# Gated mix of linear attention and a gated MLP: phi(k)'s sums by accumulating transfers, the gate's logits turned by VectorE, x's second chunk loaded later

## The chip, the cores and the metric

The kernel runs on one core of a Trainium2 chip. A core has TensorE (PE, matrix products into PSUM), VectorE (DVE), ScalarE (ACT), GpSimd (POOL) and SyncE (SP); here GpSimd and SyncE mainly issue transfers (DMAs) for the 16 DMA engines. Each engine executes its own queue in order, and waits on semaphores for the others. The metric is the device time of one execution in microseconds, the median of several runs. Next to it stands one profiled execution, in which every instruction has a start and a duration.

## The reference

Only `A_x` (2048 tokens x 640) is used as input x of both branches. Cut to what matters:

```python
x = A_x
g = sigmoid((x * gate_w).sum(-1, keepdims=True))     # one gate logit for each token
q, k, v = split(x @ wqkv)                            # 32 heads of 20 columns each
phi = lambda t: where(t > 0, t + 1, exp(t)) + 1e-6
kv = einsum("bhsd,bhse->bhde", phi(k), v)
z = phi(k).sum over the tokens                       # one number for each head and column
num = einsum("bhqd,bhde->bhqe", phi(q), kv)
den = einsum("bhqd,bhd->bhq", phi(q), z) + 1e-6
a = (num / den).reshape(1, 2048, 640) @ wo
b = (sigmoid(x @ w_gate) * (x @ w_up)) @ w_down      # 1536 inner columns
return g * a + (1 - g) * b
```

All is float32. The result is handed over transposed, as `out_t`.

## The kernel before

**Products.** Each float32 operand is split into a high and a low part (`split`: ScalarE copies the high part, VectorE subtracts it), and a product is three matmuls: high by high, high by low, low by high (`mm3`, lines 200 to 202; nearly all rows of TensorE carry one of these lines). The large products with x go by a scheme of Strassen's kind: seven products of half blocks instead of eight, on sums of quarters of x (`Chunk.sum`, `Chunk.form`, the forms `xt0` to `xt3`) and of the weights (`queue_w`: pieces G, U, S, V). `Chunk.sum(3)` and `Chunk.form(3)` make the fourth form of x.

**Stages.** (1) Up to about 145 us: k for all tokens in blocks of 128, phi(k), and G^T = x^T phi(k) into `gt`. Along the way `phi` copies one column of the product, the gate's logit, into `logit` (128 tokens by 16 blocks), and `z_add` adds the block of phi(k) to `zacc` (128 x 640) with an accumulating transfer from GpSimd's queue. (2) 145 to about 228 us: q for the two pairs of token groups (`QLast`, `QBlock`), phi(q) (`phi_q`, stored to `p_dram`), and between the blocks' steps the list `parts`: for six groups of heads `kv_part` (kv from `gt` and wv, then VectorE masks and splits it: kvt, kvh, kvl), `m_part` (kv times wo into `ms`, stored to `m_dram`), and the small work on z and the logits. `m_close` then frees the memory of this stage (`kp` with `gt` and `zacc`, `m1`, `mp`) and loads x of pair 0 again into tiles that lie there (`hf`). (3) The gated MLP's first half in 12 blocks, with the denominators made beside it (`begin`, `den`: they use `zcol` and `zeps`). (4) The second half, with kv wo as further rows of w_down.

**z and the logits before.** `z_perm` (part 2): VectorE adds the epsilons to `zacc` and permutes its columns. `z_part` (part 6): five products of `zperm` with a column of ones, line 1083, sum over the 128 partitions into the five columns of `zcol`; VectorE copies them and makes `zeps`, their sum by partition. `turn_logits` (part 2): line 1091 turns `logit` by a product with the identity `ident`, ScalarE copies it to `lt`, and GpSimd stores it to `l_dram`, from which the gates are later read by rows (`gate_row`).

**Order.** The program is unrolled, and its order is written out by hand with a planner's help. `Order` keeps estimated clocks for TensorE, ScalarE and VectorE; work is queued with estimated costs, a `ready` time and a key, and `fill` puts queued work between the matmuls when the clocks say that it fits; `need(key)` forces it. `step(blk, s)` runs step s of a block and then fills. Work that a DMA brings has an estimated due time (`est`, `later`). The DMA queues follow from this order: SyncE's carries the loads, GpSimd's the stores and accumulates. Tiles with the same tag share a ring of buffers: `ke`, `lt` and most `ms` share `ma` (two), `xnst`, every third `wv_sb`, `zperm` and every third `ms` share `mb` (two).

**Loads in stage 2.** `load_mv` brings a group's columns of wv, `load_mo` rows of wo (line 1068), `load_x1` the second chunk of x of pair 0 (`xst`, line 335); the last one is queued with a condition on how many groups of wv have been asked for:

```python
order.add(0, 0, load_x1, None, lambda: 0.0 if 3 in MV else 1e9)
```

Of the kernel before, what the change touches and what calls it, by code (L numbers as in the profile page):

```python
# [7 lines left out]
F32 = mybir.dt.float32  # L8
# [7 lines left out]
P = 128  # L16
# [161 lines left out]
def gated_mix_kernel(ctx: ExitStack, tc: tile.TileContext, xt, xn, wk, wv, wo, wst_q, wst_f, out_t):  # L178
# [64 lines left out]

    zcol = common.tile([P, KC], F32, name="zcol")
    zeps = common.tile([P, 1], F32, name="zeps")
    logit = common.tile([P, S // P], F32, name="logit")
    p_dram = dram.tile([P, KC, NG, TG], F32, name="p_dram")
    mp_dram = dram.tile([P, KC, D], F32, name="mp_dram")
    m_dram = dram.tile([D, D], F32, name="m_dram")
# [2 lines left out]
    h_dram = {(pr, n): dram.tile([P, FC // 2 + 2, TG], F32, name=f"h{pr}{n}") for pr in range(2) for n in FORMS}  # L252
    d_dram = [dram.tile([H, 2, TG], F32, name=f"d{i}") for i in range(2)]
    f_dram = dram.tile([P, TG], F32, name="f_dram")
    s_dram = [dram.tile([P, 2, TG], F32, name=f"s{p}") for p in range(FC // 2 + 2)]
    r_dram = [dram.tile([P, 2, TG], F32, name=f"r{pr}") for pr in range(2)]
    bdn = HPG * DH


    common.tile([P, 56], F32, name="space")  # L260

    kp_cm = tc.tile_pool(name="kp", bufs=1)
    kp = kp_cm.__enter__()
    gt = kp.tile([P, KC, D], F32, name="gt")
    ident = kp.tile([P, P], F32, name="ident")
    ones_f = kp.tile([P, P], F32, name="ones_f")
    bd = kp.tile([HPG * DH, HPG, DH], F32, name="bd")
    zacc = kp.tile([P, D], F32, name="zacc")
# [55 lines left out]
    class Chunk:  # L324
# [54 lines left out]
        def queue_sums(self, first=True, last=True):  # L379
            w = 2 * self.w  # L380
            plan = [(0, ()), (1, ()), (2, ((1, 3), (0, 4), (2, 5)))] if first else []
            for n, forms in plan + ([(3, ((3, 6),))] if last else []):
                order.add(0, v_cost(w), lambda n=n: self.sum(n), None, lambda: self.at)
                for t, k in forms:
                    order.add(a_cost(w), v_cost(w), lambda t=t: self.form(t), self.key(k))

        def queue(self, sums=True):
            self.queue_a()
# [239 lines left out]
    def z_add(r):  # L628

        nc.gpsimd.dma_start(zacc.rearrange(view2, j=2), r, accum_op=OP.add if z_started else OP.bypass)  # L630
        z_started.append(1)

    def queue_split(b):
        for s in range(2):
            order.add(a_cost(D), v_cost(D), lambda s=s: k_split(tok(b, s)), ("pk", b))
# [73 lines left out]
        W[n, piece] = [t[:, c] for c in range(2)]  # L709
        split(*W[n, piece], src)  # L710

    def queue_w(n, between=None, early=False):


        def raw(i, k0, k1):
            return WST[n][:, i, k0 * P:k1 * P]

        def g_part():
            w_form(n, "G", raw(0, 0, KC))
            if n[0] == "u":  # L720
                order.then(load_w)

        def sums(part):
            if part == 0:
                add(raw(1, 2, 4), raw(1, 0, 2), raw(1, 2, 4))
                sub(raw(1, 0, 2), raw(0, 0, 2), raw(1, 0, 2))
            else:
                sub(raw(0, 0, 2), raw(1, 2, 4), raw(0, 0, 2))
                sub(raw(0, 2, 4), raw(0, 2, 4), raw(0, 0, 2))
                sub(raw(0, 4, 5), raw(0, 4, 5), raw(1, 4, 5))  # L730

        def form_u():
            w_form(n, "U", raw(1, 2, KC))

        if early:
            order.add(a_cost(3 * P), v_cost(3 * P), form_u, None, lambda: max(W_AT.get(n, 1e9), w_free("U")))
            order.add(0, 2 * v_cost(2 * P), lambda: sums(0))
            return
        order.add(a_cost(D), v_cost(D), g_part, ("G", n),
                  lambda: max(W_AT.get(n, 1e9), w_free("G")))  # L740
        if n[0] != "u":
            if between:
                between()
            else:
                order.add(a_cost(3 * P), v_cost(3 * P), form_u, None, lambda: max(W_AT.get(n, 1e9), w_free("U")))
                order.add(0, 2 * v_cost(2 * P), lambda: sums(0))
            order.add(0, 3 * v_cost(2 * P), lambda: sums(1))
            order.add(a_cost(D), v_cost(D), lambda: w_form(n, "S", raw(0, 0, KC)), ("S", n),
                      lambda: w_free("S"))

# [26 lines left out]
    for k in range(2, KC):  # L777
        b1.k(k)
        if k == 2:
# [4 lines left out]
            split_xn(1)  # L784


    ij = p1.tile([P, HW], F32, name="ij", tag="ta", bufs=2)[:, :P].bitcast(I32)
    nc.gpsimd.memset(ones_f, 1.0)
    nc.gpsimd.iota(ij, pattern=[[1, P]], base=P, channel_multiplier=-1)
    nc.gpsimd.affine_select(bd, ones_f[:bdn, :bdn].rearrange("p (b c) -> p b c", c=DH),  # L790
                            pattern=[[-DH, HPG], [0, DH]], base=0, channel_multiplier=1,
                            compare_op=OP.is_ge, fill=0.0)
    nc.gpsimd.affine_select(bd, bd, pattern=[[DH, HPG], [0, DH]], base=DH - 1, channel_multiplier=-1,
                            compare_op=OP.is_ge, fill=0.0)

    def constants():
        vec1(ident, ij, float(P), op0=OP.is_equal)


    order.pe = max(order.pe, order.vec)  # L800
# [14 lines left out]
    for c in range(1, 4):  # L815
        ck = chunks[c]
        if c == 1:
            a, b = KPlain(2), KPlain(3)
            order.need((ck, "plain"))
            queue_ks()  # L820
            queue_xn(2)
            for k in range(KC):
                a.k(k)
                order.fill()
            a.phi_a()
            for k in range(KC):
                b.k(k)
                order.fill()
                if k == 0:
                    a.phi_b()  # L830
                    order.add(0, 0.6, constants)
            order.need(("ks", 5))
            for t in range(2):
                k_split(tok(2, t))
        else:
            a, b = KBlock(2 * c), KBlock(2 * c + 1)
            for n in range(1, 6):
                order.need((ck, n))
                if c == 2 and n >= 3:
                    order.need(("ks", (1, 0, 2)[n - 3]))  # L840
                getattr(a, f"s{n}")()
                getattr(b, f"s{n}")()
                if n == 2:
                    queue_xn(2 * c)
            order.need((ck, 6))
            if c == 2:
                order.need(("ks", 5))
            if c + 1 < len(chunks):
                chunks[c + 1].load()
            else:  # L850
                nx = [Chunk(0, i, None, xst_v) for i in range(2)]
                nx[0].load()
            a.s6()
            a.s7()
            a.sum_b()
            a.phi_a()
            b.s6()
            a.phi_b()
            order.need(("pk", 2 * c - 1))
            k_split(tok(2 * c, 0))  # L860
            b.s7()
            b.sum_b()
            k_split(tok(2 * c, 1))
# [30 lines left out]
        for u in range(2 * KC):  # L894
            g.part(u, 3 if u < 4 else 0, 4)
            order.fill()
    order.need(("xn", 7))
    glast = GTBatch(4, [7])
    tags = ["rot", "rot", "dd", "dd", "ch", "ch", "cc", "cc", "rot", "rot"]

    for u in range(4):
        glast.part(u, 0, 2, tags[u])
    for u in range(4, 10):
        glast.part(u, 0, 2, tags[u], out=False)
        order.fill()
    p1_tail = [lambda u=u: glast.out(u) for u in range(4, 10)]
    p1_cm.__exit__(None, None, None)

# [30 lines left out]
    class Block:  # L939
# [18 lines left out]
        def s1(self):  # L958
            order.need(("G", self.n))
            self.ch = ch_tile()  # L960
            prod(self.ch, self.terms("G", (0, 1), self.a(0, 1)), True)
            self.dd = ps_tile("dd")
            prime(self.dd)
            act(self.dd, self.ch, AF.Copy, "q" if self.n == ("q", 2) else "p")

        def s2(self):
            prod(self.dd, self.terms("G", (2, 3, 4), self.a(2, 3, 4)), False)
# [101 lines left out]
            MO[hg] = o  # L1069
            MO_AT[hg] = order.pe + 5.0  # L1070

    ZP = []

    def z_perm():
        zperm = m1_tile("mb", "zperm")
        ZP.append(zperm)
        vec1(zperm.rearrange("p (d h) -> p d h", h=H), zacc.rearrange("p (h d) -> p d h", d=DH), S // P * EPS, op0=OP.add)

    def z_part():
        zperm = ZP[0]  # L1080
        zps = ps_tile("ch")
        for u in range(KC):
            nc.tensor.matmul(zps[:, u:u + 1], zperm[:, u * P:(u + 1) * P], ones_f[:, 0:1], start=True, stop=True)
        vec_copy(zcol, zps[:, :KC], "p")
        nc.vector.tensor_reduce(zeps, zcol, op=OP.add, axis=mybir.AxisListType.X)
        vec1(zeps, zeps, EPS)

    def turn_logits():

        ps = ps_tile("rot")  # L1090
        nc.tensor.matmul(ps[:S // P, :P], logit, ident, start=True, stop=True)
        t = m1.tile([P, D], F32, name="lt", tag="ma", bufs=2)[:S // P, :P]
        act(t, ps[:S // P, :P], AF.Copy, "p")
        nc.gpsimd.dma_start(l_dram, t)

    def wo_split(hg):
        _, w = hg_slice(hg)
# [85 lines left out]
    def gate_row(g, rows=P):  # L1183
# [2 lines left out]
    nt = Chunk(0, 0, XF[0], None, TG)  # L1186


    parts = [[lambda: kv_part(0)], [lambda: kv_part(1), z_perm, turn_logits], [lambda: kv_part(2)],
             [lambda: kv_part(3), lambda: m_part(0)], [lambda: kv_part(4), lambda: m_part(1)],  # L1190
             [lambda: kv_part(5), z_part, lambda: m_part(2)], [lambda: m_part(3)], [lambda: m_part(4)],
             [lambda: m_part(5), m_rows, m_close]]

    def part():
# [28 lines left out]
    def load_x1():  # L1223
        nx[1].load(est=7.0)
        nx[1].later = 3.0
    order.add(0, 0, load_x1, None, lambda: 0.0 if 3 in MV else 1e9)
    nx[1].queue_a()
    nx[1].queue_b()
    order.stream = order.items
# [12 lines left out]
    for n, b in enumerate(blocks):  # L1242
# [11 lines left out]
        if n != 1:  # L1254
            queue_su({0: ("q", 1), 2: ("q", 2), 3: ("f", 0)}[n])
        if n == 1:
            queue_w(("q", 2), lambda: nt.queue_sums(first=False))
        elif n == 2:
            queue_w(("u", 0))
            queue_w(("f", 0))  # L1260
# [110 lines left out]
            order.late.append((max(order.pe, order.vec) + 1.0, lambda: den_sum(half, 0)))  # L1371

    def begin():
        st["a"], st["b"] = h_tile(), h_tile()
        load_pair(0)
        load_pair(1)
# [515 lines left out]
```

## Time and profile before

| what | us |
|---|---|
| median of 3 runs | 733.09 |
| lowest and highest run | 732.86, 735.78 |
| the profiled execution | 731.36 |
| its span, first to last instruction | 729.6 |
| TensorE busy | 723.1 (99%) |
| VectorE busy | 487.3 (67%) |
| ScalarE busy | 319.8 (44%) |
| GpSimd busy | 119.3 (16%) |

Matmuls overlap in the records: one of 512 columns shows about 0.39 us, and the next starts 0.23 us after it, so times on TensorE are counted from start to start. A row of the order of time gives start, duration, engine, line, operation, what is written and read, its shape and count, and in brackets how long the engine was idle before and what released it. `SPq` rows are issues by SyncE's queue. TensorE's granted clock is 0.999 of full speed over the span.

### The profile page before, as it was taken

The numbers are of one execution on the slowest core, as the hardware profiler recorded it, in microseconds if no ns is written. First come the engines' busy times: TensorE is split into PE (matmuls) and PEld (weight loads), VectorE is DVE, ScalarE is ACT, GpSimd is POOL, SyncE is SP. The second block draws the span as 40 slices with busy tenths as digits, with TensorE's granted clock in tenths as the row PEclk, the third lists the DMA queues.
The fourth block names the chain that finished last, engine by engine and source line by source line (L and its number), as shares of the span: only waits on it lengthen the run. The fifth ranks groups of instructions, "written<-read, shape, count | busy, mean of one in ns | idle before, by whom it ended". The sixth has DMA issues, their size and how long they took to land.

```text
span 729.6 us, 9792 instructions
## 1 busy us (share of the span) xinstructions
PE 723.1 (99%) x3552; PEld 619.5 (85%) x3552; DVE 487.3 (67%) x787; ACT 319.8 (44%) x540; POOL 119.3 (16%) x207
## 2 busy tenths in 40 slices
PE   9999999999999999999999999999999999999997
PEld 7999999988878888888888888888888888888886
DVE  4878566867764688678879868795856764434340
ACT  5764627156766324233423342233356654424320
POOL 0211010111311023212224223240200000010000
PEclk9999999999999999999999999999999999999999
DMA  8453537587636454755587658475887965465432
GB/s 265 116 137 88 154 54 233 111 257 263 206 131 222 152 195 130 206 187 199 213 280 276 237 182 286 164 260 161 282 315 260 341 220 198 154 214 191 150 113 73
DMA packets 61941, 143.67 MB, mean 197 GB/s; under 512 B 10798, under 2 KB 23870, under 8 KB 61893
## 3 DMA queue, kind: packets, MB, share of 16 engines
q1 hardware_dynamic: 43685, 88.50, 37.8%
q0 software_dynamic: 18064, 54.42, 22.8%
q8 instruction: 28, 0.46, 0.3%
q14 instruction: 20, 0.16, 0.1%
q10 hardware_dynamic: 144, 0.13, 0.1%
HBM read 89.73 MB, written 49.68 MB: 191 GB/s over the span
## 4 chain that ended last, share of the span: by engine, by line
PE 96%; DMA 2%; DVE 1%; ACT 1%; issue 0%; SPq 0%; DVEq 0%
PE ch L202 9%; PE ch L201 9%; PE ch L200 9%; PE cc L200 9%; PE cc L201 8%; PE cc L202 8%; PE rot L200 8%; PE rot L201 8%; PE rot L202 8%; PE dd L200 6%; PE dd L201 6%; PE dd L202 6%; DMA wo_sb<-wo 1%; DMA xnh<-wk 0%; DVE wol L216 0%; ACT woh L212 0%
## 5 line engine op out<-in xcount | busy, mean ns | idle before, releaser
L216 DVE TENSOR_TENSOR hf<-hw,hf 128x1024 fp32r<-128x1024 f32 x54 | 65.9, 1223 | 68.9 <-ACT hf L212 68.5
L212 ACT ACTIVATE hf<-hw 128x1024 fp32r<-128x1024 f32 x54 | 56.9, 1057 | 62.3 <-PE rot L202 31.2
L216 DVE TENSOR_TENSOR c<-cc,c 128x512 f32<-128x512 f32 x56 | 37.8, 686 | 45.7 <-PE cc L202 41.3
L212 ACT ACTIVATE wG<-wst 128x640 fp32r<-128x640 f32 x17 | 12.4, 737 | 65.0 <-PE dd L202 65.0
L212 ACT ACTIVATE c<-ch 128x512 f32<-128x512 f32 x32 | 19.1, 598 | 49.3 <-PE ch L202 44.5
L1688 POOL DMA_DIRECT2D out_t<-ot x18 | 9.7, 541 | 182.4 <-DVE ot L216 179.3
L200 PE MATMUL dd<-xrh,wG 128*128 128x512 f32 x90 | 35.6, 395 | 0.0
L202 PE MATMUL dd<-xrh,wG 128*128 128x512 f32 x90 | 35.0, 389 | 0.0
L201 PE MATMUL dd<-xrl,wG 128*128 128x512 f32 x90 | 35.0, 389 | 0.0
L216 DVE TENSOR_TENSOR c<-c,om 128x512 f32<-128x512 f32 x48 | 33.2, 692 | 1.7
L200 PE MATMUL cc<-xbh,wS 128*128 128x512 f32 x84 | 32.8, 390 | 0.1
L201 PE MATMUL cc<-xbl,wS 128*128 128x512 f32 x84 | 32.7, 389 | 0.0
L202 PE MATMUL cc<-xbh,wS 128*128 128x512 f32 x84 | 32.7, 389 | 0.0
L200 PE MATMUL rot<-pkh,xnh 128*128 128x320 f32 x102 | 31.7, 310 | 0.0
L201 PE MATMUL rot<-pkl,xnh 128*128 128x320 f32 x102 | 31.5, 309 | 0.0
L202 PE MATMUL rot<-pkh,xnl 128*128 128x320 f32 x102 | 31.4, 308 | 0.0
L200 PE MATMUL dd<-hf,wa 128*128 128x512 f32 x80 | 31.1, 389 | 0.0
L201 PE MATMUL dd<-hf,wa 128*128 128x512 f32 x80 | 31.1, 389 | 0.0
L202 PE MATMUL dd<-hf,wa 128*128 128x512 f32 x80 | 31.1, 389 | 0.0
L200 PE MATMUL ch<-hf,wa 128*128 128x512 f32 x80 | 31.1, 389 | 0.0
L201 PE MATMUL ch<-hf,wa 128*128 128x512 f32 x80 | 31.1, 389 | 0.0
L202 PE MATMUL ch<-hf,wa 128*128 128x512 f32 x80 | 31.1, 389 | 0.0
(471 smaller groups left out, 2211.5 us busy)
## 6 DMA issues: line engine op xcount, KB each, us to landing
hf<-p_dram SPq DMA_DIRECT2D x16, 512.0 KB, 4.7
hw<-h1T SPq DMA_DIRECT2D x16, 512.0 KB, 4.9
hw<-h0T SPq DMA_DIRECT2D x16, 512.0 KB, 4.6
wst<-wst_f SPq DMA_DIRECT2D x12, 640.0 KB, 4.3
xst<-xt SPq DMA_DIRECT2D x10, 640.0 KB, 7.0
h1T<-c POOLq DMA_DIRECT2D x24, 256.0 KB, 2.7
h0T<-c POOLq DMA_DIRECT2D x24, 256.0 KB, 3.5
hw<-h1B SPq DMA_DIRECT2D x11, 512.0 KB, 4.5
```

The lines of the kernel that those rows point to most:

```text
L200: nc.tensor.matmul(out, l_hi, r_hi, start=first, stop=False, skip_group_check=True)
L201: nc.tensor.matmul(out, l_hi, r_lo, start=False, stop=False, skip_group_check=True)
L202: nc.tensor.matmul(out, l_lo, r_hi, start=False, stop=last, skip_group_check=True)
L212: nc.scalar.activation(out, src, fn, **kw)
L216: nc.vector.tensor_tensor(out, a, b, op=op)
L1688: (eng or nc.gpsimd).dma_start(out_t[o * P:(o + 1) * P, g * TG + c0:g * TG + c1], t[:, c0:c1])
```

## The change

1. *z*: the tile `zperm`, `z_perm` and `z_part` go. In their place `z_step`, called nine times, works off a list: seven accumulating transfers add the upper half of the rows that are left of `zacc` to the lower half (64 rows, 32, down to 1), an eighth call stores row 0 to `z_dram`, a ninth loads it by four transfers into the five columns of `zcol`. All are issued by GpSimd. The calls stand after the fifth and ninth product of the third batch's last loop, after the second, sixth and tenth of the last batch, and in parts 1, 2, 3 and 5. `z_done`, at the start of stage 3, adds the epsilons and makes `zeps`.
2. *Logits*: the identity and the instructions that make it go. `logit` is 32 columns wide (the upper 16 are zeros); VectorE turns its four blocks of 32 x 32 at once, and four transfers instead of one store them.
3. *x's second chunk*: `load_x1` waits for the fifth group of wv to be asked for, not the fourth; it moves behind the loads of wo and wv of that part.
4. *Order of the group ("q", 2)*: x's fourth sum stays ahead of the weights' last three sums, the fourth form is queued behind them.
5. The copy in `Block.s1` names the pair too in its condition for the wait "q". The tile `space` shrinks by as much as `logit` grows.

```diff
-    logit = common.tile([P, S // P], F32, name="logit")
+    logit = common.tile([P, 32], F32, name="logit")
+    z_dram = dram.tile([1, D], F32, name="z_dram")
-    common.tile([P, 56], F32, name="space")
+    common.tile([P, 40], F32, name="space")
-    ident = kp.tile([P, P], F32, name="ident")
...
+        def queue_sum3(self):
+            order.add(0, v_cost(2 * self.w), lambda: self.sum(3), None, lambda: self.at)
+
+        def queue_form3(self):
+            order.add(a_cost(2 * self.w), v_cost(2 * self.w), lambda: self.form(3), self.key(6))
...
+    z_tree = [64, 32, 16, 8, 4, 2, 1, 0, -1]
+
+    def z_step():
+        n = z_tree.pop(0)
+        if n > 0:
+            nc.gpsimd.dma_start(zacc[:n], zacc[n:2 * n], accum_op=OP.add)
+        elif n == 0:
+            nc.gpsimd.dma_start(z_dram, zacc[0:1])
+        else:
+            for d in range(4):
+                nc.gpsimd.dma_start(zcol[d * H:(d + 1) * H], z_dram.rearrange("o (h u d) -> (o d) h u", u=KC, d=4)[d])
...
-    def queue_w(n, between=None, early=False):
+    def queue_w(n, between=None, early=False, third=None):
...
             order.add(0, 3 * v_cost(2 * P), lambda: sums(1))
+            if third:
+                third()
             order.add(a_cost(D), v_cost(D), lambda: w_form(n, "S", raw(0, 0, KC)), ("S", n),
...
-    ij = p1.tile([P, HW], F32, name="ij", tag="ta", bufs=2)[:, :P].bitcast(I32)
+    nc.gpsimd.memset(logit[:, S // P:], 0.0)
-    nc.gpsimd.iota(ij, pattern=[[1, P]], base=P, channel_multiplier=-1)
-    def constants():
-        vec1(ident, ij, float(P), op0=OP.is_equal)
-                    order.add(0, 0.6, constants)
...
             g.part(u, 3 if u < 4 else 0, 4)
             order.fill()
+            if c == 3 and u in (4, 8):
+                z_step()
...
         glast.part(u, 0, 2, tags[u])
+        if u == 1:
+            z_step()
     for u in range(4, 10):
         glast.part(u, 0, 2, tags[u], out=False)
         order.fill()
+        if u in (5, 9):
+            z_step()
...
-            act(self.dd, self.ch, AF.Copy, "q" if self.n == ("q", 2) else "p")
+            act(self.dd, self.ch, AF.Copy, "q" if (self.pr, self.n) in ((0, ("q", 2)),) else "p")
...
-    def z_perm():
-        zperm = m1_tile("mb", "zperm")
-        vec1(zperm.rearrange("p (d h) -> p d h", h=H), zacc.rearrange("p (h d) -> p d h", d=DH), S // P * EPS, op0=OP.add)
-    def z_part():
-        for u in range(KC):
-            nc.tensor.matmul(zps[:, u:u + 1], zperm[:, u * P:(u + 1) * P], ones_f[:, 0:1], start=True, stop=True)
-        vec_copy(zcol, zps[:, :KC], "p")
+    def z_done():
+        vec1(zcol, zcol, S * EPS, op0=OP.add)
         nc.vector.tensor_reduce(zeps, zcol, op=OP.add, axis=mybir.AxisListType.X)
         vec1(zeps, zeps, EPS)
 
     def turn_logits():
-        ps = ps_tile("rot")
-        nc.tensor.matmul(ps[:S // P, :P], logit, ident, start=True, stop=True)
-        t = m1.tile([P, D], F32, name="lt", tag="ma", bufs=2)[:S // P, :P]
-        act(t, ps[:S // P, :P], AF.Copy, "p")
-        nc.gpsimd.dma_start(l_dram, t)
+        t = m1.tile([P, D], F32, name="lt", tag="ma", bufs=2)[:, :32]
+        nc.vector.transpose(t, logit)
+        order.on_vec(32, "")
+        for r in range(0, P, 32):
+            nc.gpsimd.dma_start(l_dram[:, r:r + 32], t[r:r + S // P])
...
-    parts = [[lambda: kv_part(0)], [lambda: kv_part(1), z_perm, turn_logits], [lambda: kv_part(2)],
-             [lambda: kv_part(3), lambda: m_part(0)], [lambda: kv_part(4), lambda: m_part(1)],
-             [lambda: kv_part(5), z_part, lambda: m_part(2)], [lambda: m_part(3)], [lambda: m_part(4)],
+    parts = [[lambda: kv_part(0), z_step], [lambda: kv_part(1), turn_logits, z_step], [lambda: kv_part(2), z_step],
+             [lambda: kv_part(3), lambda: m_part(0)], [lambda: kv_part(4), lambda: m_part(1), z_step],
+             [lambda: kv_part(5), lambda: m_part(2)], [lambda: m_part(3)], [lambda: m_part(4)],
              [lambda: m_part(5), m_rows, m_close]]
...
-    order.add(0, 0, load_x1, None, lambda: 0.0 if 3 in MV else 1e9)
+    order.add(0, 0, load_x1, None, lambda: 0.0 if 4 in MV else 1e9)
...
-            queue_w(("q", 2), lambda: nt.queue_sums(first=False))
+            queue_w(("q", 2), nt.queue_sum3, third=nt.queue_form3)
...
     def begin():
+        z_done()
```

More of the change, by code (lines that the diff above doesn't have):

```diff
@@ L1070, in load_mo @@
             MO_AT[hg] = order.pe + 5.0
-    ZP = []
-    def z_perm():
-        zperm = m1_tile("mb", "zperm")
-        ZP.append(zperm)
-        vec1(zperm.rearrange("p (d h) -> p d h", h=H), zacc.rearrange("p (h d) -> p d h", d=DH), S // P * EPS, op0=OP.add)
-    def z_part():
-        zperm = ZP[0]
-        zps = ps_tile("ch")
-        for u in range(KC):
-            nc.tensor.matmul(zps[:, u:u + 1], zperm[:, u * P:(u + 1) * P], ones_f[:, 0:1], start=True, stop=True)
-        vec_copy(zcol, zps[:, :KC], "p")
+    def z_done():
+        vec1(zcol, zcol, S * EPS, op0=OP.add)
         nc.vector.tensor_reduce(zeps, zcol, op=OP.add, axis=mybir.AxisListType.X)
```

## The prediction

> **What bounds the kernel.** I read the page first, then TensorE's waits, then the stretch from 136 to 210 us in order of time, because everything the diff touches that TensorE executes lies there.
>
> ```profile
> span 729.6 us, 9792 instructions
> ...
> PE 723.1 (99%) x3552; PEld 619.5 (85%) x3552; DVE 487.3 (67%) x787; ACT 319.8 (44%) x540; POOL 119.3 (16%) x207
> ...
> PE 96%; DMA 2%; DVE 1%; ACT 1%; issue 0%; SPq 0%; DVEq 0%
> ```
>
> TensorE is busy for 723.1 of 729.6 us and holds 96% of the chain that ended last. So only two things can change the time by much: matmuls that are added or removed, and stalls of TensorE. The list of its waits is short:
>
> ```profile
> PE rot L290 <- POOL warm L287: 1.4, 1, 1.4
> PE cc L1114 <- DVE kvl L216: 0.5, 1, 0.5
> PE ch L202 <- DVE wS L216: 0.3, 1, 0.3
> ```
>
> The first is the start of the program. The other two lie in the stretch that the change rearranges. Everything else that the diff moves (VectorE's copies, GpSimd's and SyncE's transfers) counts only if it makes TensorE wait.
>
> **Matmuls removed.** In order of time on TensorE:
>
> ```profile
> 150.95 0.39 PE L1091 MATMUL rot<-ident,logit 128*16 128x128 f32 x2
> 151.27 0.50 PE L200 MATMUL ch<-xbh,wG 128*128 128x512 f32 x1
> 164.54 1.27 PE L1083 MATMUL ch<-ones_f,zperm 128*128 128x1 f32 x10
> 165.67 0.39 PE L200 MATMUL rot<-woh,kvh 120*120 120x320 f32 x1
> ```
>
> Matmuls overlap, so I count from start to next start: the logits' turn costs 151.27 - 150.95 = 0.32 us, the five column sums of z 165.67 - 164.54 = 1.13 us. Together 1.45 us leave TensorE, with nothing put in their place there. On VectorE the permuting of zacc, the copy of zcol and the identity go, a transpose and one small addition come; VectorE is 67% busy and this is under 1 us either way, so I count it as nothing as long as it is not the last to arrive. The change of the copy's wait in the first step of the blocks costs nothing: it names group 2 of q in pair 0, and that group occurs in no other pair.
>
> **x's second chunk is loaded one part later.** The wait for kvl has this history:
>
> ```profile
> 148.39 1.61 SPq L335 DMA_DIRECT2D xst<-xt  x2
> 150.13 1.01 SPq L1068 DMA_DIRECT2D wo_sb<-wo  x2
> 158.12 0.74 ACT L212 ACTIVATE woh<-wo_sb 120x640 fp32r<-120x640 f32 x1 [2.02 <-DMA wo_sb<-wo]
> 158.89 0.82 DVE L216 TENSOR_TENSOR wol<-wo_sb,woh 120x640 fp32r<-120x640 f32 x1 [2.07 <-ACT woh L212]
> 160.56 1.28 PE cc L1114 x10
> ```
>
> The columns are start, duration, instruction (the last row is the chain's). The two loads of x (640 KB each) go out just ahead of two loads of wo; ScalarE then waits for wo, VectorE for ScalarE, and kvt, kvh and kvl queue behind it. How long such a load of wo takes without and with x in front:
>
> ```profile
> wo_sb<-wo SPq DMA_DIRECT2D x1, 300.0 KB, 3.0
> wo_sb<-wo SPq DMA_DIRECT2D x2, 300.0 KB, 8.3
> ```
>
> The first row is the first load of wo in this stretch, ahead of x, the second the pair at 150.13. With x behind wo and the next wv, I expect wo some 4 us earlier, and the wait gone: 0.5 us, plus the restart seen in the gap before 160.56, say 0.6. The ends are 0 (something else holds VectorE there) and 0.7. What is late next is x itself: issued at about 152 instead of 148.4, landing near 160. Its first use by TensorE is the first step of the third block:
>
> ```profile
> 185.28 0.39 PE L200 MATMUL ch<-xah,wG 128*128 128x512 f32 x1
> ```
>
> So there is cover of over 20 us; without it each us would count.
>
> **The order of the third weight group.** The wait for wS:
>
> ```profile
> 200.65 1.23 DVE L216 TENSOR_TENSOR xt3l<-hf,xt3h 128x1024 fp32r<-128x1024 f32 x1 [1.61 <-ACT xt3h L212]
> 201.80 1.08 DVE L216 TENSOR_TENSOR wst<-wst 128x256 f32<-128x256 f32 x3
> 206.21 0.50 PE L202 MATMUL ch<-xt1h,wS 128*128 128x512 f32 x1 [0.31 <-DVE wS L216]
> ```
>
> Today x's fourth form precedes the weight's last sums, and those three (1.08 us) follow it. After the change they come first, and fit into the 1.61 us in which VectorE waits for ScalarE. wS can then be ready some 1 us earlier, and the 0.3 us go. Ends: 0.3 gained, 0.3 lost if the form is now the late one.
>
> **phi(k)'s sums by transfers.** This is where the change can lose. Seven accumulating transfers (64 rows down to 1), a store and four small loads are added to GpSimd's queue; each of the first eight waits for the one before, and whatever is queued behind it on GpSimd waits too. In the order of issue: five steps before the first part, step 6 (2 rows) in the first part, then the first store of phi(q), then four stores of the turned logits in place of one, step 7, the second store of phi(q), step 8 (the store of z), then m's first store. GpSimd's rows today:
>
> ```profile
> 136.30 1.22 POOL L630 DMA_DIRECT2D zacc<-kb  x1 [3.46 <-DVE wG L216]
> 152.73 0.68 POOL L1094 DMA_DIRECT2D l_dram<-lt  x1
> 161.02 0.56 POOL L1135 DMA_DIRECT2D m_dram<-ms  x1 [3.33 <-ACT ms L212]
> ```
>
> Times from issue to landing, in us at the end of each row: of zacc's last sum, of the first store of phi(q) (issued just ahead of l_dram's), of l_dram's and of m's first:
>
> ```profile
> zacc<-kb POOLq DMA_DIRECT2D x1, 320.0 KB, 4.2
> p_dram<-qr POOLq DMA_DIRECT2D x1, 256.0 KB, 7.5
> l_dram<-lt POOLq DMA_DIRECT2D x1, 8.0 KB, 7.1
> m_dram<-ms POOLq DMA_DIRECT2D x1, 300.0 KB, 3.6
> ```
>
> The tree can begin at 136.3 + 4.2 = 140.5. A step of it is shown nowhere. Above it stands an accumulate of 128 KB among other transfers:
>
> ```profile
> 261.39 0.52 POOL L1384 DMA_DIRECT2D d<-hf  x1 [14.00 <-DVE hf L220]
> 266.50 0.86 POOL L1384 DMA_DIRECT2D d<-hf  x1 [0.43 <-DMA d<-hf]
> DMA to landing us min/median/max: 1.7/4.2/6.8
> ```
>
> The first two rows are an issue and the next one that waited for it, 5.1 us later; the third is that tile's summary, with 1.7 us as its shortest. So a step lies between 1.7 and 5.1 us. Its surroundings differ:
>
> ```profile
> 140.00:144.00 4.00, 4.00 (x28) 3.94 (x27) 3.16 (x8) 2.17 (x4) 0.00 (x0) 1.00 0.00 0
> 148.00:152.00 4.00, 4.00 (x24) 3.23 (x23) 3.12 (x7) 2.07 (x5) 0.00 (x0) 1.00 0.98 300
> ```
>
> The last two columns are the DMA engines' busy share and GB/s: idle at first, full later. I take 3.1 us on the average, a us below the 4.2 of the full zacc for fewer bytes. Five steps end at 140.5 + 15.5 = 156.0. Then step 6 and the first store of phi(q) go out, then the four logit stores at some 0.6 us each, until 159.6; behind a store of 256 KB they land near 164 (7.5 us after that store's issue at 156.6, as now).
>
> Who waits for that? The turned logits lie in the buffer that the second group's product ms takes next but one, and ScalarE writes it in the first of these rows (the second comes up below):
>
> ```profile
> 162.37 0.82 ACT L212 ACTIVATE ms<-rot 120x320 f32<-120x320 f32 x2 [0.32 <-ACT xah L212]
> 169.37 0.83 ACT L212 ACTIVATE ms<-rot 120x320 f32<-120x320 f32 x2 [0.63 <-ACT xbh L212]
> ```
>
> Today the logits have landed by 152.73 + 7.1 = 159.8. After the change ScalarE stands at ms until 164, its PSUM buffer is free 0.4 us later, and the next group's product, which would now start at 165.67 less the 2.4 us gained = 163.3, starts at about 164.4: 1.1 us lost. The bounds: 0 with steps under 2.9 us, and 7 us with the last three steps at 5.1 (below).
>
> The price per step has a rule to weigh. The Trainium skill (DMA: Bandwidth & Descriptors, section Anatomy of one DMA — SWDGE (gpsimd) path) gives about 2.0 us fixed plus bytes at 436 GB/s for each such transfer. By that, an estimate, the five steps take 2.4 + 2.2 + 2.1 + 2.05 + 2.0 = 10.8 us, ScalarE waits for nothing and the sum is that of the first rival. The trace so far disagrees: by the same rule zacc's 320 KB would take 2.8 us and its row says 4.2.
>
> Step 8 holds m's first store back until about 165; plus 3.6 it lands at 168.7, when ScalarE, now at 169.37, would want that buffer near 168: under 1 us, hidden by what TensorE then has queued. And x's next pair is loaded into memory that holds zacc:
>
> ```profile
> 166.90 3.99 SPq L335 DMA_DIRECT2D hf<-xt  x4
> 187.30 1.23 DVE L216 TENSOR_TENSOR xt1l<-hf,xt1h 128x1024 fp32r<-128x1024 f32 x1 [1.13 <-ACT xt1h L212]
> 192.76 0.39 PE L200 MATMUL ch<-xt1h,wS 128*128 128x512 f32 x1
> ```
>
> It must now wait for the store of z, which lands near 167. TensorE first uses these forms 192.76 - 188.53 = 4.2 us after they are made, so up to 4 us more would still be covered.
>
> **Sum.** -1.45 (matmuls) - 0.6 (kvl) - 0.3 (wS) + 1.1 (ms) = -1.25 us. It is made on the profiled execution, 731.36 us with a span of 729.6; the median of the runs, 733.09, lies 1.7 above. Taken off the median: 731.8 us.
>
> **Rivals.** *The tree is quick.* With steps at 2.5 us the logits land before 162 and nothing waits: -2.35, 730.7 us. For it speaks the idle DMA at 140 to 144 and the shortest landing of 1.7; against it the full DMA after 148.
>
> *The tree is slow, and the kernel slower.* One mechanism: the logits' store behind it holds ms. Steps of 3.3 and 3.4 and three of 5.1 end at 162.5; the first store of phi(q) and the logits go out until 165.6 and land near 170.5; TensorE loses 7 us, net +4.7: 737.8 us. It decides from a landing past 169.4, which is 6.1 us lost. Against it: transfers of a few rows have little to share with SyncE's loads.
>
> *Only the matmuls count.* The new order of loads and sums moves the two stalls instead of removing them, with ms still at 1.1: -0.35, 732.7 us.
>
> **Chances.** The forecast 0.50, the quick tree 0.23, only the matmuls 0.12, the slow tree 0.15. 0.5% is 3.7 us, about what a measurement of this kernel can tell from no change. Faster by more needs 729.4, that is all of the quick case and another us that no row shows: 0.06. Slower by more takes the slow case and a little of a new stall that I have not seen: 0.17. The rest, 0.77, is no change. The range reaches from the quick tree with a us to spare, 729.4, to the edge of the slow one, 736.3.
>
> **What the profile after would show.** No row for the matmuls of lines 1083 and 1091; no wait of TensorE for kvl near 160 or for wS near 206; seven issues on zacc between 140 and 165 us, some 3 us apart; ScalarE waiting at ms for l_dram's transfer, and TensorE a us behind it. The prediction is wrong if those issues lie 5 us apart, if the first store of phi(q) goes out after 160, if x's next pair is loaded after 171, or if TensorE shows waits outside 140 to 210 us.

## The result and the profile after

The changed kernel takes 740.02 us in the median of six runs, beside 733.14 for the kernel before: a ratio of 1.0088 over the runs, 95% interval 1.0068 to 1.0108. It is slower, by 6.9 us, and outside the forecast range. The profiled execution took 739.75 us with this span:

```profile
span 737.9 us, 9798 instructions
...
PE 724.7 (98%) x3540; PEld 620.3 (84%) x3540; DVE 486.5 (66%) x786; ACT 319.4 (43%) x539; POOL 128.8 (17%) x222
```

TensorE's waits (total, count, longest):

```profile
PE rot L200 <- ACT ms L212: 6.6, 1, 6.6
PE rot L290 <- POOL warm L287: 1.4, 1, 1.4
PE ch L200 <- ACT c L212: 0.6, 1, 0.6
PE rot L201 <- DVE pkl L220: 0.6, 1, 0.6
```

The two waits that stood here before, for kvl and for wS, are gone, as forecast. In their place stands one of 6.6 us, at a product that writes a PSUM buffer which ScalarE has not emptied into ms. ScalarE's rows there:

```profile
162.53 0.64 ACT L212 ACTIVATE xah<-xst 128x512 fp32r<-128x512 f32 x1
171.09 0.77 ACT L212 ACTIVATE ms<-rot 120x320 f32<-120x320 f32 x2 [7.92 <-DMA l_dram<-lt]
```

It waited 7.9 us for the store of the turned logits, whose buffer ms takes over. GpSimd's queue shows why that store was late:

```profile
142.94 0.86 POOL L645 DMA_DIRECT2D zacc<-zacc  x1 [3.23 <-DMA zacc<-kb]
146.15 0.79 POOL L645 DMA_DIRECT2D zacc<-zacc  x1 [2.34 <-DMA zacc<-zacc]
152.94 0.77 POOL L645 DMA_DIRECT2D zacc<-zacc  x1 [6.00 <-DMA zacc<-zacc]
158.68 0.80 POOL L645 DMA_DIRECT2D zacc<-zacc  x1 [4.98 <-DMA zacc<-zacc]
163.68 0.82 POOL L645 DMA_DIRECT2D zacc<-zacc  x1 [4.19 <-DMA zacc<-zacc]
166.23 0.77 POOL L645 DMA_DIRECT2D zacc<-zacc  x1 [1.73 <-DMA zacc<-zacc]
166.93 0.69 POOL L1033 DMA_DIRECT2D p_dram<-qr  x1
167.56 2.00 POOL L1105 DMA_DIRECT2D l_dram<-lt  x4
...
171.88 0.50 POOL L647 DMA_DIRECT2D z_dram<-zacc  x1 [0.90 <-DMA zacc<-zacc]
172.39 0.56 POOL L1146 DMA_DIRECT2D m_dram<-ms  x1
```

The steps of the tree are 3.2, 6.8, 5.7, 5.0 and 2.6 us apart. The first store of phi(q) goes out at 166.93 (152.13 before), the logits' at 167.56 (152.73), m's first at 172.39 (161.02). What sets a step's length is seen when the same stretches are asked for the DMA engines' load. In these rows stand the stretch, its length, the busy time of TensorE, its weight loads, VectorE, ScalarE and GpSimd, then TensorE's granted clock, the DMA engines' busy share and GB/s:

```profile
142.94:146.15 3.21, 3.21 (x22) 3.08 (x21) 2.84 (x6) 2.18 (x4) 0.86 (x2) 1.00 0.33 51
146.15:152.94 6.79, 6.79 (x42) 5.95 (x41) 5.66 (x12) 4.39 (x8) 0.79 (x2) 1.00 0.93 256
163.68:166.23 2.55, 1.34 (x14) 0.83 (x12) 1.01 (x4) 0.00 (x0) 0.82 (x2) 1.00 0.04 4
```

160 KB took 3.2 us at a busy share of 0.33, 80 KB took 6.8 at 0.93. The stall has a tail, which TensorE's granted clock shows, four us to a row:

```profile
164.00:168.00 4.00, 1.02 (x13) 0.54 (x11) 0.69 (x3) 0.00 (x0) 2.27 (x4) 1.00 0.04 4
168.00:172.00 4.00, 0.42 (x1) 0.42 (x2) 0.00 (x0) 0.91 (x3) 3.10 (x7) 0.67 0.34 116
172.00:176.00 4.00, 4.00 (x13) 3.42 (x13) 3.39 (x9) 3.71 (x7) 3.44 (x7) 0.50 0.60 155
176.00:180.00 4.00, 4.00 (x23) 3.62 (x22) 1.34 (x2) 0.83 (x2) 1.99 (x4) 0.98 0.99 324
```

During the wait the clock fell to half, and the first four us after it ran at 0.50: 2 us more lost. The span is 8.3 us longer than before: 6.6 for ms, 2.0 for the clock, 0.6 for c, less 1.45 of matmuls and 1.2 of the two old stalls (counted as gaps between starts, 0.7 and 0.5). That leaves some 1.7, by which TensorE was behind before anything of the changed stretch began: the first kv product starts at 148.40 (146.67 before), after small delays up to 122 us, the wait for pkl among them. The kernel of the first experiment is the same up to there, shows no wait for pkl and starts that product at 147.52, so I do not charge that wait to the change; where the other 0.9 comes from stays open.

### The profile page after: what moved, and what is told of

The parts are those of the page before. It is cut to its first block, busy times and chain, and to the rows that moved or that the text cites. A ratio compares the mean times of both kernels' runs of the same rounds, so it can differ in the third digit from the quotient of the medians.

```text
span 737.9 us, 9798 instructions
## 1 busy us (share of the span) xinstructions
PE 724.7 (98%) x3540; PEld 620.3 (84%) x3540; DVE 486.5 (66%) x786; ACT 319.4 (43%) x539; POOL 128.8 (17%) x222
## 4 chain that ended last, share of the span: by engine, by line
PE 76%; DMA 5%; ACT 1%; DVE 1%; issue 1%; POOL 0%; ACTq 0%; DVEq 0%
PE cc L200 7%; PE cc L201 7%; PE cc L202 7%; PE ch L200 7%; PE ch L201 7%; PE ch L202 7%; PE rot L201 6%; PE rot L200 6%; PE rot L202 6%; PE dd L200 5%; PE dd L201 5%; PE dd L202 5%; DMA zacc<-zacc 3%; DMA wo_sb<-wo 1%; DMA xnst<-xn 1%; DMA zacc<-kb 1%
```

## Experiments

The theory after the result: the tree holds GpSimd's in-order queue, its steps being slow while the DMA engines are full, and TensorE stalls through whatever stands behind it. Rivals: the shared buffer alone; x's later load or the four logit stores; the transfers' own traffic.

**The logits in a buffer of their own.**

```diff
-        t = m1.tile([P, D], F32, name="lt", tag="ma", bufs=2)[:, :32]
+        t = m1.tile([P, 32], F32, name="lt", tag="lt", bufs=1)
```

> The changed kernel, but the turned logits get a buffer of their own, so ScalarE's ms no longer waits for their store. Queue theory (the tree of z holds GpSimd's in-order queue, and everything behind it is late): the wait of ScalarE at the second ms (7.9 us in the changed kernel) goes, but m's first store still stands behind the store of z, at about 172 us, and lands near 175.5, so ScalarE now waits some 5 us at the fourth ms for m_dram's transfer; 736 to 739 us. Buffer theory (only the shared buffer of the logits is at fault): no wait of more than 1 us is left, 730.5 to 732.5 us.

740.22 us, ratio 1.0096 (1.0059 to 1.0134). TensorE's wait, ScalarE's and the rows of GpSimd's queue:

```profile
PE rot L200 <- ACT ms L212: 7.4, 1, 7.4
```

```profile
176.90 0.77 ACT L212 ACTIVATE ms<-rot 120x320 f32<-120x320 f32 x2 [9.23 <-DMA m_dram<-ms]
```

```profile
173.23 0.50 POOL L647 DMA_DIRECT2D z_dram<-zacc  x1 [0.90 <-DMA zacc<-zacc]
173.74 0.56 POOL L1146 DMA_DIRECT2D m_dram<-ms  x1
```

The buffer theory falls. The stall only moves on, two groups later, to m's store behind the store of z, the place that the queue theory named. Its sizes were too small: ScalarE waited 9.2 us where some 5 were expected, and 740.22 lies above the 736 to 739. Up to that stall, with the tree's first six transfers in their place, TensorE waited 0.5 us between 140 and 170 us, so their traffic alone stalls it little.

**No tree.** z by TensorE as before; the three other edits stay.

```diff
-    parts = [[lambda: kv_part(0), z_step], [lambda: kv_part(1), turn_logits, z_step], [lambda: kv_part(2), z_step],
+    parts = [[lambda: kv_part(0)], [lambda: kv_part(1), z_perm, turn_logits], [lambda: kv_part(2)],
...
-             [lambda: kv_part(5), lambda: m_part(2)], [lambda: m_part(3)], [lambda: m_part(4)],
+             [lambda: kv_part(5), z_part, lambda: m_part(2)], [lambda: m_part(3)], [lambda: m_part(4)],
```

The calls in the batches before go too.

> The changed kernel, but z is summed by TensorE as before; the logits' transpose, x's later load and the order of the third weight group stay. Queue theory: the loss goes entirely, and the matmul of the logits (0.3 us), the wait for kvl (0.6) and the wait for wS (0.3) stay saved: about 731.9 us, 731 to 733. Rival (x's later load or the four logit stores share the blame): over 735 us, with a wait of TensorE between 155 and 185 us.

731.1 us, ratio 0.9971 (0.9951 to 0.9991): faster than before. TensorE's list of waits is down to the program's start:

```profile
PE rot L290 <- POOL warm L287: 1.4, 1, 1.4
```

So the whole loss is the tree's, and the other edits together gain.

**The tree alone,** on the kernel before.

```diff
-    parts = [[lambda: kv_part(0)], [lambda: kv_part(1), z_perm, turn_logits], [lambda: kv_part(2)],
+    parts = [[lambda: kv_part(0), z_step], [lambda: kv_part(1), turn_logits, z_step], [lambda: kv_part(2), z_step],
```

That is one of the three lines of `parts`. `z_step`, `z_done` and the nine calls are those of the change; the old `turn_logits` and the old order of loads and sums stay.

> The kernel before with the tree of z alone; logits turned by TensorE and stored in one transfer, x's second chunk early. Queue theory: the same stall at ms, since the logits' store still stands behind six steps of the tree: 738 to 742 us. Rival (x's later load is what slows the tree's steps): the steps are some 3 us, the sixth is issued by 158 us, and the time is 731 to 734 us.

739.47 us, ratio 1.0084 (1.005 to 1.0118), with a single logit store and x early. TensorE's two longest waits, and the second and third steps' stretches:

```profile
PE rot L200 <- ACT ms L212: 6.3, 1, 6.3
PE cc L1123 <- DVE kvt L216: 1.8, 1, 1.8
```

```profile
152.43:160.43 8.00, 7.74 (x47) 6.61 (x45) 0.98 (x2) 1.40 (x3) 0.78 (x1) 1.00 0.93 243
160.43:163.11 2.68, 1.15 (x11) 1.15 (x11) 2.15 (x5) 2.68 (x7) 0.77 (x1) 1.00 0.36 51
```

x's later load and the four stores are not to blame. The slow steps lie where x is now: 8.0 us at a share of 0.93, 2.7 at 0.36.

**Other queues for what stands behind the tree.**

```diff
-            nc.gpsimd.dma_start(l_dram[:, r:r + 32], t[r:r + S // P])
+            nc.sync.dma_start(l_dram[:, r:r + 32], t[r:r + S // P])
...
-        nc.gpsimd.dma_start(m_dram[c0:c0 + w], ms[:w])
+        nc.scalar.dma_start(m_dram[c0:c0 + w], ms[:w])
```

> The changed kernel, but the four stores of the logits go out from SyncE's queue and the stores of m from ScalarE's, so none of them stands behind the tree; phi(q)'s stores stay on GpSimd. Queue theory: no wait of TensorE above 1 us between 140 and 190 us, and what was saved stays saved: 730.5 to 732.5 us. Rival (the transfers themselves are slow beside the tree, whichever queue issues them): ScalarE still waits several us at ms, 735 us or more.

734.26 us, ratio 1.001 (0.9993 to 1.0027). The stall at ms is gone, but not all of the time is back, and the time lies between the two forecasts:

```profile
PE cc L1125 <- DMA wv_sb<-wv: 3.5, 1, 3.5
```

```profile
158.61 0.34 SPq L1090 DMA_DIRECT2D wo_sb<-wo  x1
163.14 0.40 SPq L1083 DMA_DIRECT2D wv_sb<-wv  x1
```

SyncE's load of the last wv, which followed wo's at once in the changed kernel, went out 4.5 us after it. In the list of SyncE's waits its line stands so:

```profile
SPq L1083 <- DMA m_dram<-ms: 4.2, 1, 4.2
```

The store of m that ScalarE issued at 160.09 took 3.0 us to land, so it ends when the load goes out. The logits' stores, issued on SyncE's queue between 153.3 and 156.8, needed up to 6.1 us to land, which is about the same time, so which of the two moved stores held the load stays open. The new wait is for a load of SyncE's, and neither theory had it. The clock fell here too, and was at 0.50 from 166 to 172.

**The tree late.** Two steps stand as they were (the second takes 6.0 us to land here, which is before the store behind it is due); then, behind the logits' stores, 32 rows go to DRAM, and the other five steps add up there between the steps of the q blocks.

```diff
+    z_tree = [64, 32, 0, 16, 8, 4, 2, 1, -1]
...
         elif n == 0:
+            nc.gpsimd.dma_start(z_dram, zacc[:32])
+        elif n > 0:
+            nc.gpsimd.dma_start(z_dram[:n], z_dram[n:2 * n], accum_op=OP.add)
...
         step(b, 4)
         part()
+        if n:
+            z_step()
...
             step(nxt or last, 2)
+            if n:
+                z_step()
```

> The changed kernel, but only the first two steps of the tree stand where they were; after the logits' stores the 32 rows left are stored to DRAM, and the other five steps add up there, issued one by one between the steps of the q blocks, some 6 us apart, after the stores of m. Queue theory: nothing that ScalarE or SyncE needs stands behind a waiting step, so no wait of TensorE above 1 us is left and all 1.45 us of matmuls are saved on top of the other gains: 730 us, 729 to 731.5. Rival (the tree costs by its transfers): over 733 us.

730.49 us, ratio 0.9967 (0.9954 to 0.998), with all nine calls of the tree still there. Two rows of GpSimd and TensorE's longest wait:

```profile
192.19 0.79 POOL L648 DMA_DIRECT2D z_dram<-z_dram  x1 [5.61 <-DMA z_dram<-z_dram]
192.73 0.84 POOL L1030 DMA_DIRECT2D p_dram<-qr  x1
```

```profile
PE cc L1122 <- DMA wv_sb<-wv: 1.4, 1, 1.4
```

A step still makes GpSimd's queue wait 5.6 us, and a store of phi(q) behind it, and TensorE does not notice. So a waiting step costs by what stands behind it: here nothing that TensorE soon needs. As the last five steps run in another stretch here, this run alone does not price their traffic where the change has them. The expectation that no wait above 1 us is left was missed by the 1.4 for wv.

**x later still,** in the changed kernel.

```diff
-    order.add(0, 0, load_x1, None, lambda: 0.0 if 4 in MV else 1e9)
+    order.add(0, 0, load_x1, None, lambda: 0.0 if 5 in MV else 1e9)
```

> The changed kernel, but x's second chunk is loaded one part later still, behind the load of the sixth group of wv. If the tree's steps are slow because they share the DMA engines with SyncE's loads, the third to fifth steps get faster: the sixth is issued by 162 us (166.2 in the changed kernel), TensorE's wait for ms shrinks from 6.6 to 2 to 4 us, 734 to 737 us. If the steps are slow by themselves, the sixth stays at 165 to 168 us and the time at 739 to 741.

742.29 us, ratio 1.013 (1.011 to 1.015): my numbers for it were wrong. The profiled execution, at 739.05, is the fastest of the four, so the rows below do not explain the whole median. SyncE's load of x, GpSimd's rows from the fourth step, and the two stretches between them:

```profile
159.76 1.25 SPq L335 DMA_DIRECT2D xst<-xt  x2
```

```profile
157.79 0.80 POOL L645 DMA_DIRECT2D zacc<-zacc  x1 [3.92 <-DMA zacc<-zacc]
160.46 0.79 POOL L645 DMA_DIRECT2D zacc<-zacc  x1 [1.87 <-DMA zacc<-zacc]
166.13 0.77 POOL L645 DMA_DIRECT2D zacc<-zacc  x1 [4.88 <-DMA zacc<-zacc]
```

```profile
157.79:160.46 2.67, 2.67 (x19) 2.38 (x19) 2.60 (x7) 1.26 (x3) 0.80 (x1) 1.00 0.23 36
160.46:166.13 5.67, 4.66 (x38) 4.01 (x36) 3.32 (x10) 1.85 (x4) 0.79 (x2) 1.00 0.94 282
```

The fourth step did get fast, 2.7 us where it was 5.0; then x's load went out at 159.8, and the fifth, with half the rows, took 5.7 where it was 2.6. The slowness moved with the load. So the steps' price is the DMA engines' load, but moving one load only moved it to another step. The sixth step still went out at 166.1, which is the number of the other branch (steps slow by themselves); the quick fourth step, at a share of 0.23, speaks against that branch. VectorE does not set the price either: it was busy for 2.60 of 2.67 us beside the quick step, and for 3.32 of 5.67 beside the slow one.

**x early, without the tree.** The fourth group's condition as before (`3 in MV`), one execution.

> The kernel without the tree, with x's second chunk loaded as early as before. If the wait of TensorE for kvl hung on x's load standing ahead of wo's, it is back: 0.4 to 0.7 us at the fourth kv product, near 160 us. If it hung on something else, it stays away.

735.6 us. A wait is back at the fourth kv product, larger, and with wv's load as its releaser, not kvl:

```profile
PE cc L1130 <- DMA wv_sb<-wv: 2.3, 1, 2.3
```

That load, behind x, took 9.5 us to land, against 5.2 in the kernel without a tree, where x stands behind it. The clock, by single us (last three columns: clock, DMA share, GB/s):

```profile
161.00:162.00 1.00, 0.00 (x0) 0.00 (x0) 0.68 (x1) 1.00 (x3) 0.00 (x0) 1.00 0.12 44
164.00:165.00 1.00, 1.00 (x6) 1.00 (x5) 0.93 (x4) 0.47 (x1) 0.00 (x0) 0.50 1.14 294
167.00:168.00 1.00, 1.00 (x9) 0.59 (x8) 0.93 (x4) 0.69 (x2) 0.80 (x2) 0.96 0.17 66
```

**The old order of the third group, without the tree.** `queue_w(("q", 2), lambda: nt.queue_sums(first=False))` again, one execution.

> The kernel without the tree, with x's fourth form ahead of the weights' last sums as before. If the wait of TensorE for wS hung on that order, it is back: 0.2 to 0.5 us near 205 us. If not, it stays away.

731.21 us, and exactly the old wait, at 204.9 us:

```profile
PE ch L202 <- DVE wS L216: 0.3, 1, 0.3
```

The time does not tell the two orders apart: it lies within the runs of the kernel without a tree, 729.9 to 733.04.

**The late tree with x later still.** The two edits together.

> The kernel with the late tree, and x's second chunk loaded behind the sixth group of wv. There TensorE waited 1.4 us for the load of wv issued at 158.25, which ran beside x's load. If x's load is what slows wo's and wv's, this wait goes and nothing takes its place, since x is first used near 185: 729.2 us, 728.5 to 730. If it is only a matter of chance between executions, 730 to 731.

730.24 us, ratio 0.9965 (0.9952 to 0.9978). The wait for wv is gone, as expected if x's load is the cause, but the time is in the other branch's range, and a wait of 0.5 us for ms has come:

```profile
PE rot L200 <- ACT ms L212: 0.5, 1, 0.5
```

This kernel, the late tree and the one without a tree all beat both kernels of the case; their intervals overlap, and the runs do not rank them.

## Why the prediction was wrong

*The bound* was right: TensorE, and the change counts through added work and stalls alone.

*Matmuls removed, 1.45 us:* nothing here contradicts it, but no run measured it by itself. The kernel without a tree keeps 1.13 of it on TensorE and is as fast, within the intervals, as the ones with the late tree.

*x's second chunk, 0.6 us:* half right. Loads behind x are slow (wo took 8.3 us before and 5.0 in the changed kernel), and the wait for kvl went. But with the other edits in and x early, the wait that comes back is at wv's load, which I had not priced, and not at kvl; in the one execution it was 2.3 us.

*The third group's order, 0.3 us:* right by the wait, which comes and goes with it; 0.3 us is too little for the times to show.

*phi(k)'s sums* is the step that failed: the term for ms stood at 1.1 us, and the runs show 6.6 us of waiting and 2.0 for the clock. Two things under it were wrong. First, the price of a step: I took 3.1 us on the average between bounds of 1.7 and 5.1, and the five steps took 3.2, 6.8, 5.7, 5.0 and 2.6, on the average 4.7. I had quoted the row that the DMA engines are full from 148 on, and then weighted the idle stretch; above all I took one row of an accumulate beside other transfers, 5.1 us, for an upper bound, though the steps beside full engines went to 6.8 and, with x early, to 8.0. My own rows went further: the summary of that tile has 6.8 as its longest landing, of which I used only the shortest, and the 8 KB of l_dram took 7.1. The argument against the slow tree, that transfers of a few rows have little to share with SyncE's loads, is answered by x later still, where 10 KB took 5.7 us from issue to next issue beside such loads. The sixth step was issued at 166.2, not at 156.0: 2.4 us of that are the chain's later start (142.94, not 140.5), 7.8 the five steps. The Trainium skill (DMA: Bandwidth & Descriptors, section Anatomy of one DMA — SWDGE (gpsimd) path) has some 2.0 us fixed, plus the bytes at 436 GB/s. The trace agrees with that only where the engines are idle:

```profile
zacc<-zacc POOLq DMA_DIRECT2D x1, 80.0 KB, 6.5
zacc<-zacc POOLq DMA_DIRECT2D x1, 5.0 KB, 2.0
```

Those are the second and the sixth step's times to landing.

Second, what a stall costs. I priced the wait for ms at the wait alone. Its mechanism, place and order in the queue were those of the slow-tree rival, which gave 737.8 us and a chance of 0.15; but the clock's fall added 2 us that no term of mine held. The Trainium skill (TensorE: Matmul & The Clock Gate, section Why this matters for your kernels) warns of idle gaps above some 3 us, after which the clock is at half; the trace agrees with a wait of 6.6 us and a clock of 0.50. A shorter one was enough with x early, where 0.50 followed a wait of 2.3 us, and there the measurement decides.

*m's first store:* I called it hidden, at under 1 us. With the logits out of the way it was the next stall, 7.4 us. Both came from the same mis-sized chain. Three of the signs that I had named came with it: issues 5 us apart and more, phi(q)'s first store after 160 (166.93), x's next pair after 171 (174.13).

## What to carry to other kernels

In this kernel a chain of transfers that wait for each other was priced by the load of the DMA engines where it ran more than by its bytes, and its cost was paid by what stood behind it on its issuing queue. Before placing such a chain, list those followers and their waiters, and place it where none is urgent. The chain cost 1.2% in one place (ratio 1.0088 with it, 0.9971 without) and nothing measurable with its last five steps in DRAM, 32 to 39 us later (0.9967). When a TensorE stall of more than some 2 us is a possible outcome, price it with the half-speed stretch that follows it.

## What was not expected of the hardware

Transfers of 40 and 20 KB took 5.7 and 5.0 us from issue to next issue beside SyncE's loads, against 2.6 for 10 KB beside idle engines. And the clock falls late and stays low: in the changed kernel TensorE stopped at about 165 us, the mean clock was still 1.00 up to 168 and then fell, and it was back only after 176, over 4 us after the matmuls had resumed at 171.6. The delay is not fixed: with x later still TensorE stopped at 165.1, and the clock was at 0.55 already between 167 and 168. In the kernel with x early and no tree, a wait of only 2.3 us was enough: the clock was still 1.00 during it and 0.50 from 164 to 167, with TensorE busy; the late tree's wait of 1.4 us left it at 1.00.
